# The fifth key block of the value product in high and low parts, weights widened by integer addition, and a new order of steps

## The chip, the cores and the metric

The kernel runs on one core of a Trainium2 chip, as one program. The metric is the device time of an execution in microseconds (us), the median of three runs. The engines are named as in the profile: PE (TensorE, matmul), PEld (its weight load), DVE (VectorE), ACT (ScalarE), POOL (GpSimd) and SP (SyncE, which issues most DMAs).

## The reference

Three parts stand one behind the other; the output of each is the input of the next.

```python
# q, k, v: (2, 8, 576, 64); rotary on q and k, softmax over 576 keys
scores = scale * np.matmul(q_rot, k_rot.transpose(0, 1, 3, 2))
attn = np.exp(scores - np.max(scores, axis=-1, keepdims=True))
attn = attn / (np.sum(attn, axis=-1, keepdims=True) + 1e-09)
x = np.matmul(attn, v)            # -> (1152, 512)
h = x @ w_in                      # (512, 2048), float64
x = (h * sigmoid(h)) @ w_out      # (2048, 512), float64
p = domain_probs / (domain_probs.sum(-1, keepdims=True) + 1e-09)
for e in range(4):                # w1[e]: (512, 1024), w2[e]: (1024, 512)
    out += p[:, e:e + 1] * (np.maximum(x @ w1[e], 0.0) @ w2[e])
```

## The kernel before

Every product that needs full precision is made of float32r numbers in two parts: a high part `hi` (a rounded copy) and a low part `lo` (the number less `hi`); a product is then two or three matmuls.

Attention goes over 8 pairs of heads. A pair has 9 units: four row blocks of 128 queries for each of its two heads, and one unit (h = 2) in which the last 64 queries of both heads lie together. So there are 72 iterations. In iteration `i` the kernel issues the scores of unit i + 2 (`scores`, PE, L401 to L413), their row maximum (`rowmax`, DVE, L420), the exponential of unit i + 1 (`expo`, ACT, L430), and for unit i the transposes of the probabilities (`transp`, PE, L306) with the high copy on ACT (L468) and the low subtraction on DVE (L473). Background work of neighbouring pairs is put in between: transposes of the next pair's rotated queries and keys (`qkt_*`), the product with the values (`av`), normalising (`norm`), and on POOL the rotary of the pair after next.

Three things set the order. `PLAN*` says in which of the nine iterations of a pair a background item stands. `ORDER*` is one string for each of the nine iterations: each letter issues one group of steps (S scores, M maximum, E exponential, T transposes, H high copies, L low halves, B background, v and V copies out of PSUM, X delayed steps). POOL's items are dealt out at a steady rate. Every engine runs its instructions in the order in which they were issued. `PLAN0` and `ORDER0` belong to the first pair, `PLAN2` and `ORDER2` to the last two.

The 576 keys of a head are four blocks of 128 and a fifth block of 64. For the four, `av` multiplies `P.V` (values, high in one half of the 128 columns and low in the other) with `pth` and `ptl`, the high and low parts of the transposed probabilities: eight matmuls of 256 or 320 columns (L503). The fifth block is not split: plain float32 values `V5` (64 rows for each head) and probabilities `p5`, two matmuls on 64 rows and 64 columns, each on one half of the query columns (L509). `p5` comes from one transpose into a bank of its own behind every unit with h = 1, and one copy on ACT (L470). The pool `ps1` has four PSUM banks for all of this.

The weights `w_in` and `w_out` are float64. `widen` turns the two 32-bit halves `hw` and `lw` of 512 numbers for each partition into a high and a low float32r part: 7 operations on DVE and 2 on ACT (L90 to L112). The first quarter of `w_in` is widened during attention in four slices, which start in the iterations 15, 24, 33 and 51 of `CONV` and take one stage in each iteration from there. The rest follows in the two expert stages.

Of the kernel before, what the change touches and what calls it, by code (L numbers as in the profile page):

```python
# [7 lines left out]
F32 = mybir.dt.float32  # L8
# [28 lines left out]
def fused_kernel(ctx, tc, q, k, v, w_in, w_out, dprobs, w1, w2, cst, out):  # L37
    nc = tc.nc
# [22 lines left out]
    wslot = [None] * 4  # L61

# [20 lines left out]
    def widen(cv, raw, wh, wl, slow=False):  # L83
# [33 lines left out]
        if slow:  # L117
            return [together(t0, t1), together(t2, t3, t4), t5, together(t6, t7)]
# [34 lines left out]
    pp = apool(ectx, "pp", 2)  # L153
# [10 lines left out]
    V5 = [hold5.tile([128, 64], F32, name=f"v5_{i}") for i in range(2)]  # L164
# [50 lines left out]

    def load_v5(P):
        if P.n >= 2:
            for h in range(2):
                assert (pairs[P.n - 2], "avmm", 1, h) in made
        for h in range(2):  # L220
            nc.sync.dma_start(V5[P.i][64 * h:64 * h + 64, :], v[P.b, 2 * P.hp + h, 512:576, :])
# [54 lines left out]
    def vsplit(P):  # L276
# [156 lines left out]
    def transp(P, un):  # L433
        hf, r, h = un
        if (r, h) == (P.halves[hf][0], 0):
# [4 lines left out]
                pool.tile([128, W], F32, name="p5"),  # L440
# [47 lines left out]
    def av(P, hf, h):  # L488
# [3 lines left out]
        def mm(i):  # L492
# [31 lines left out]
        return [(W / 2400, lambda i=i: mm(i)) for i in range(9)]  # L524
# [804 lines left out]
```

## Time and profile before

| | us |
|---|---|
| median of 3 runs | 766.76 (766.74 to 767.05) |
| the profiled execution | 765.77 |
| its span in the trace | 764.0 |
| PE busy | 747.0 (98%) |
| DVE busy | 508.9 (67%) |
| ACT busy | 341.7 (45%) |
| POOL busy | 286.6 (38%) |

Attention takes the first 187 us or so; the two expert stages follow. Busy shares are means over both, so they say little of either: the windows further down cut attention into pairs. Matmul records overlap (one starts before the one ahead has ended), so how long a matmul holds PE is read from the distance of two starts, not from its duration.

### The profile page before, as it was taken

The page shows a single profiled execution, that of the slowest core. Times are in us where ns is not written, and L with a number is a line of the kernel's source. Part 1 is how long each engine was busy: PE and PEld are TensorE (multiplying, and loading weights), DVE is VectorE, ACT ScalarE, POOL GpSimd, SP SyncE. Part 2 cuts the span into 40 slices and gives each one's busy share as a digit, 9 for nine tenths or more (in the row PEclk, how much of TensorE's full clock was granted, in tenths as well). Part 3 has the DMA queues.
Part 4 walks back from the last instruction along what each step waited for, and adds up shares of the span by engine and source line. Part 5 has one row for each costly group of instructions (what it writes and reads, how often), then busy time and mean ns, then how long its engine had stood idle before and what let it go on. Part 6 is the DMA issues. An engine that isn't in the chain of part 4 may idle for free.

```text
span 764.0 us, 12106 instructions
## 1 busy us (share of the span) xinstructions
PE 747.0 (98%) x4610; PEld 690.2 (90%) x4610; DVE 508.9 (67%) x936; ACT 341.7 (45%) x806; POOL 286.6 (38%) x308
## 2 busy tenths in 40 slices
PE   7998999999999999999999999999999999999998
PEld 6887878788999999999998898989989899898996
DVE  5789998987999899895565454545445454454542
ACT  4888888885533525235233242423314233141330
POOL 7997877421001303105331703426043261422600
PEclk8999999999999999999999999999999999999999
DMA  4445534230313133131110110301103030020002
GB/s 130 121 132 129 128 87 117 66 117 2 112 55 111 56 111 111 56 111 55 56 56 1 56 56 0 111 1 57 55 2 110 1 94 18 25 87 1 1 28 96
DMA packets 31129, 51.88 MB, mean 68 GB/s; under 512 B 7184, under 2 KB 14112, under 8 KB 31072
## 3 DMA queue, kind: packets, MB, share of 16 engines
q1 hardware_dynamic: 28720, 50.05, 21.6%
q10 hardware_dynamic: 2224, 0.79, 0.4%
q8 instruction: 36, 0.59, 0.3%
q0 software_dynamic: 128, 0.28, 0.1%
q14 instruction: 21, 0.17, 0.1%
HBM read 41.40 MB, written 2.36 MB: 57 GB/s over the span
## 4 chain that ended last, share of the span: by engine, by line
PE 89%; DVE 5%; POOL 2%; ACT 2%; issue 1%; DMA 1%; POOLq 0%; ACTq 0%; DVEq 0%
PE m L837 9%; PE m L838 9%; PE m L839 9%; PE m L766 7%; PE m L764 7%; PE m L765 7%; PE b L306 4%; PE m L648 4%; PE m L673 4%; PE m L649 4%; PE m L672 4%; PE m L650 4%; PE m L671 4%; PE b L503 3%; PE s L401 3%; ACT p L430 1%
## 5 line engine op out<-in xcount | busy, mean ns | idle before, releaser
L843 DVE SCALAR_TENSOR_TENSOR acc<-m,dp,acc 128x512 f32<-128x512 f32 (+1 forms) x64 | 47.5, 742 | 108.3 <-PE m L839 108.3
L838 PE MATMUL m<-wl,gh 128*128 128x512 f32 (+1 forms) x292 | 113.2, 388 | 0.0
L837 PE MATMUL m<-wh,gh 128*128 128x512 f32 (+1 forms) x292 | 113.1, 387 | 0.0
L839 PE MATMUL m<-wh,gl 128*128 128x512 f32 (+1 forms) x292 | 112.7, 386 | 0.0
L785 DVE SCALAR_TENSOR_TENSOR gl<-g,gh 128x288 fp32r<-128x288 f32 x84 | 51.2, 609 | 44.5 <-ACT gh L784 43.4
L747 POOL TENSOR_TENSOR wl<-raw,wh 128x512 fp32r<-128x512 f32 x21 | 27.2, 1295 | 141.5 <-ACT wh L744 141.5
L660 POOL TENSOR_TENSOR gl<-g,gh 128x384 fp32r<-128x384 f32 x24 | 26.9, 1121 | 141.3 <-ACT gh L659 112.7
L764 PE MATMUL m<-xh,wh 128*128 128x288 f32 x224 | 66.1, 295 | 0.0
L766 PE MATMUL m<-xh,wl 128*128 128x288 f32 x224 | 66.0, 295 | 0.0
L765 PE MATMUL m<-xl,wh 128*128 128x288 f32 x224 | 65.9, 294 | 0.0
L839 PEld LDWEIGHTS m<-wh,gl 128*128 128x128 f32 x292 | 54.9, 188 | 11.4
L837 PEld LDWEIGHTS m<-wh,gh 128*128 128x128 f32 x292 | 54.8, 188 | 10.7
L673 PE MATMUL m<-gl,wh 128*128 128x384 f32 x192 | 64.2, 334 | 0.0
L672 PE MATMUL m<-gh,wl 128*128 128x384 f32 x192 | 64.1, 334 | 0.0
L671 PE MATMUL m<-gh,wh 128*128 128x384 f32 x192 | 64.1, 334 | 0.0
L838 PEld LDWEIGHTS m<-wl,gh 128*128 128x128 f32 x292 | 54.8, 188 | 10.3
L747 POOL TENSOR_TENSOR wl<-cvt,wh 128x512 fp32r<-128x512 f32 x28 | 36.2, 1294 | 69.7 <-ACT wh L744 69.7
L420 DVE TENSOR_REDUCE nm<-s 128x1 f32<-128x576 f32 x72 | 53.9, 748 | 9.6 <-PE s L401 6.4
L744 ACT CAST wh<-cvt 128x512 fp32r<-128x512 f32 x28 | 17.4, 621 | 89.4 <-DVE cvt L743 89.4
L430 ACT ACTIVATE p<-s,nm 128x576 f32<-128x576 f32 x72 | 54.1, 751 | 5.6 <-DVE nm L420 5.0
L306 PE MATMUL b<-cs,p 128*128 128x128 f32 x329 | 50.5, 282 | 5.0 <-DVE xn L563 1.9
L473 DVE TENSOR_TENSOR ptl<-b,pth 128x512 fp32r<-128x512 f32 x72 | 48.8, 685 | 5.3 <-ACT pth L468 4.2
(179 smaller groups left out, 2094.6 us busy)
## 6 DMA issues: line engine op xcount, KB each, us to landing
raw<-in_moe_w_dram SPq DMA_DIRECT2D x16, 1024.0 KB, 5.1
raw<-in_moe_w_out_dram SPq DMA_DIRECT2D x8, 1024.0 KB, 5.0
raw<-in_moe_w_in_dram SPq DMA_DIRECT2D x6, 1024.0 KB, 5.0
kh<-kkh SPq DMA_DIRECT2D x28, 128.0 KB, 2.3
kl<-kkl SPq DMA_DIRECT2D x28, 128.0 KB, 2.3
xv<-in_v_dram SPq DMA_DIRECT2D x8, 256.0 KB, 2.7
raw<-in_moe_w_in_dram SPq DMA_DIRECT2D x4, 512.0 KB, 4.0
xk<-in_k_dram SPq DMA_DIRECT2D x7, 256.0 KB, 2.9
```

The lines of the kernel that those rows point to most:

```text
L306: nc.tensor.matmul(o, lhsT, idn[:, 0:n], is_transpose=True, start=True, stop=True)
L430: nc.scalar.activation(o.rearrange("p (a b) -> p a b", a=2), s[:, :, 0:288], AF.Exp, bias=P.nm[:, c:c + 1], scale=1.0, accum_out=P.sm[:, c ...
L671: nc.tensor.matmul(o, wh[:, f, ds], gh[:, cols], start=(f == 0), stop=False)
L672: nc.tensor.matmul(o, wl[:, f, ds], gh[:, cols], start=False, stop=False)
L673: nc.tensor.matmul(o, wh[:, f, ds], gl[:, cols], start=False, stop=(f == FT - 1))
L747: nc.gpsimd.tensor_tensor(lo, src(name), f32(hi), ALU.subtract)
L764: nc.tensor.matmul(ps, wh[:, k, ms], hh[:, k, cols], start=(first and k == 0), stop=False, skip_group_check=not first)
L765: nc.tensor.matmul(ps, wh[:, k, ms], hl[:, k, cols], start=False, stop=False, skip_group_check=not first)
L766: nc.tensor.matmul(ps, wl[:, k, ms], hh[:, k, cols], start=False, stop=(k == 1), skip_group_check=not first)
L837: nc.tensor.matmul(ps, gh[:, ts], wh[:, f, ds], start=(f == 0), stop=False)
L838: nc.tensor.matmul(ps, gh[:, ts], wl[:, f, ds], start=False, stop=False)
L839: nc.tensor.matmul(ps, gl[:, ts], wh[:, f, ds], start=False, stop=(f == FT - 1))
```

## The change

The fifth block of the product with the values is made like the other four: `P.V` gets a fifth block, into which `vsplit` puts high and low parts of `V5`, where each head has its own 64 rows and the other 64 rows are zero; `p5` gets a high and a low part for both heads' rows together, so that two matmuls of the full shape replace the two small ones. Its transposes are gathered: two row blocks at a time, into one bank, at units (1, 1) and (3, 1). The pool of probabilities `pp` has three buffers instead of two.

`widen0` is a new way to widen, for the four slices in attention alone: the low words become an integer on ACT, and one integer addition adds them to the shifted high words; 5 operations on DVE and 3 on ACT. `WIDE` says in which iteration the load and each of the six steps of a slice stand, and the new letter W issues them. The tables `PLAN*` and `ORDER*` are new; one line of each kind stands here.

```diff
-PLAN = [['Nk', 'L0'], [], ['Nq0', 'L1'], ['Ln'], ['P0'], ['Nr'], [], ['Nq1', 'P1'], ['Pn']]
+PLAN = [[], ['L0', 'Nk'], ['Nq0', 'L1'], ['Ln'], ['P0'], ['Nr', 'Nq1'], [], ['P1'], ['Pn']]
-ORDER = ['TvHSMEXVBL', 'SvTEBHVXML', 'vSTHEVMXBL', 'vSEVTBMXHL', 'THEvSVXMBL', 'vSVETHXMBL', 'vVSTEHMLXB', 'vTHSXLBEMV', 'vTSEXHVMBL']
+ORDER = ['ETvSMXHVWLB', 'BSETvVMHWXL', 'vTHEXSMLBVW', 'vESVMTHBLWX', 'vTWESHVXMBL', 'vTVSEBMHXWL', 'EvVSTHMWLXB', 'THvSXMLEWBV', 'vSVXTBMEHLW']
-CONV = [15, 24, 33, 51, 58, 61, 69]
+WIDE = [[24, 27, 27, 28, 28, 29, 32], [32, 34, 34, 36, 37, 40, 41], [41, 44, 44, 45, 46, 47, 50], [50, 52, 52, 53, 54, 55, 60]]
+CONV = [69]
-RB0 = 4
-VS = 6
-GEXTRA = 0.0
+RB0 = 5
+VS = 8
+GEXTRA = 0.5
...
+        def t0():
+            T["t"] = cv.tile([128, 512], U32, name="cvt", tag="cv")
+            T["y"] = cv.tile([128, 512], U32, name="cvy", tag="cv")
+            nc.scalar.activation(f32(T["t"]), f32(hw), AF.Abs)
+            nc.scalar.activation(T["y"][:], lw, AF.Identity, scale=2.0 ** -29, bias=big[:, 0:1])
+
+        def t1():
+            t = T["t"]
+            V.tensor_scalar(f32(t), f32(t), 2.0 ** -15, None, ALU.max)
+            V.tensor_scalar(t[:], t[:], 3, 0x3FFFFFF8, ALU.logical_shift_left, ALU.bitwise_and)
+
+        def t2():
+            V.scalar_tensor_tensor(T["t"][:], hw, 0xC0000000, T["t"][:], ALU.bitwise_and, ALU.bitwise_or)
+
+        def t3():
+            V.tensor_tensor(T["t"][:], T["t"][:], T["y"][:], ALU.add)
+
+        def t4():
+            nc.scalar.activation(wh, f32(T["t"]), AF.Copy, scale=0.5)
+
+        def t5():
+            V.scalar_tensor_tensor(wl, f32(T["t"]), 0.5, f32(wh), ALU.mult, ALU.subtract)
...
-    pp = apool(ectx, "pp", 2)
+    pp = apool(ectx, "pp", 3)
...
+        part(V5[P.i][:], lambda: P.V[:, :, 4, 0:64], lambda: P.V[:, :, 4, 64:128])
...
-        five = h > 0
-        W5 = 64 if h == 2 else 128
+        five = {(1, 1): (0, 1), (3, 1): (2, 3), (4, 2): (4,)}.get((r, h))
...
-                p5 = bank(128)
-                tr(p5, pr[:, 512:640])
+                p5 = bank(256)
+                for i, r5 in enumerate(five):
+                    tr(p5[:, 128 * i:128 * i + 128], P.plist[r5][:, 512:640])
...
             nc.vector.tensor_tensor(lo, src, f32(hi), ALU.subtract)
+            if five:
+                nc.vector.tensor_tensor(lo5, p5, f32(hi5), ALU.subtract)
...
-            if i < 8:
-                nc.tensor.matmul(T["ps"], P.V[:, h, i // 2, :], (pth, ptl)[i % 2][:, h, i // 2, 0:W],
-                                 start=(i == 0), stop=False)
-            else:
-                rows = slice(64 * h, 64 * h + 64)
-                for a in range(2):
-                    part = slice(a * W // 2, (a + 1) * W // 2)
-                    nc.tensor.matmul(T["ps"][64 * a:64 * a + 64, part], V5[P.i][rows, :], pt5[rows, part],
-                                     start=False, stop=True)
...
+            j, z = divmod(i, 2)
+            rhs = (pth, ptl)[z][:, h, j, 0:W] if j < 4 else pt5[:, z, :]
+            nc.tensor.matmul(T["ps"], P.V[:, h, j, :], rhs, start=(i == 0), stop=(i == 9))
```

What the change does to two of the engines, shown at two places. First PE, the product with the values for the second half of pair 2's queries, first head, as it is issued early in pair 3 (L503 and L509 become L535; `p_1026` and `p_1024` are the fifth block of the probabilities, `yk` the next pair's keys, `s` the scores). Before:

```order
L306 MATMUL b<-cs,yk 128x128 x4
L503 MATMUL b<-pth,V 128x320
L503 MATMUL b<-ptl,V 128x320
...
L503 MATMUL b<-ptl,V 128x320
L509 MATMUL b<-p_1026,v_0_114 64x160 x2
L401 MATMUL s<-kh_119,Q 128x288 x2
```

After:

```order
L535 MATMUL b<-pth,V 128x320
L535 MATMUL b<-ptl,V 128x320
...
L535 MATMUL b<-ptl,V 128x320
L535 MATMUL b<-p_1024,V 128x320 x2
L332 MATMUL b<-cs,yk 128x128 x4
L427 MATMUL s<-kh_120,Q 128x288 x2
```

The two matmuls with `V5` (here `v_0_114`) are gone, two of the full shape stand in their place, and the transposes of the keys moved from ahead of the product to behind it.

Second DVE at the same place of the program, from the end of pair 2 into pair 3, where both kernels widen a slice (before: L97, L100, L103, L109 and L112, behind L91 and L94 a few rows earlier; after: L98, L99, L102, L105; the lower half L111 follows further on). `nm` is the row maximum, `ptl` a lower half of the probabilities, `xu` the product with the values out of PSUM. Before:

```order
L484 RECIPROCAL rs<-rs 128x5
L97 TENSOR_SCALAR cvt<-cvt 128x512
L100 TENSOR_SCALAR cvt<-cvt 128x512
L103 SCALAR_TENSOR_TENSOR cvt<-raw_1109,cvt 128x512
L420 TENSOR_REDUCE nm<-s 128x1
L563 TENSOR_TENSOR xn<-xu,b 128x256
L473 TENSOR_TENSOR ptl<-b,pth 128x4x128
L333 TENSOR_TENSOR kkl<-b,kkh 128x512
L522 TENSOR_TENSOR xu<-b,tmp 64x320
L420 TENSOR_REDUCE nm<-s 128x1
L473 TENSOR_TENSOR ptl<-b,pth 128x4x128
L109 TENSOR_SCALAR raw_1109<-cvt 128x512
```

After:

```order
L504 TENSOR_TENSOR p_1024<-b,p_1024 128x64
L513 TENSOR_REDUCE rs<-sm_113 128x5
L515 RECIPROCAL rs<-rs 128x5
L446 TENSOR_REDUCE nm<-s 128x1
L587 TENSOR_TENSOR xn<-xu,b 128x256
L98 TENSOR_SCALAR cvt<-cvt 128x512
L99 TENSOR_SCALAR cvt<-cvt 128x512
L502 TENSOR_TENSOR ptl<-b,pth 128x4x128
L546 TENSOR_TENSOR xu<-b,tmp 64x320
L359 TENSOR_TENSOR kkl<-b,kkh 128x512
L446 TENSOR_REDUCE nm<-s 128x1
L102 SCALAR_TENSOR_TENSOR cvt<-raw_1107,cvt 128x512
```

The widening moved behind a row maximum and is cut into pieces, and the lower half of the fifth block (L504) is a new operation; the integer addition (L105, one custom operation on 1024 two-byte elements) comes right behind the last row shown.

## Rows read from the trace of the kernel before

**Rows 1.** Page, slices: PE's busy tenths in 40 equal slices.

```profile
PE   7998999999999999999999999999999999999998
```

**Rows 2.** Windows, pairs 1 to 7: PE, PEld, DVE, ACT, POOL busy (instructions); clock, DMA.

```profile
32.29:52.70 20.41, 20.14 (x162) 17.62 (x161) 17.25 (x32) 17.92 (x47) 19.75 (x23) 1.00 0.54 149
52.70:74.57 21.87, 19.98 (x152) 17.17 (x152) 21.01 (x37) 18.39 (x48) 18.11 (x19) 1.00 0.46 116
74.57:96.74 22.17, 20.40 (x157) 17.46 (x157) 21.30 (x38) 18.47 (x47) 16.53 (x18) 1.00 0.44 112
96.74:118.79 22.05, 20.25 (x155) 17.36 (x154) 20.44 (x37) 17.89 (x46) 16.59 (x18) 1.00 0.37 89
118.79:138.68 19.89, 19.78 (x158) 17.46 (x156) 16.76 (x31) 17.74 (x47) 15.34 (x19) 1.00 0.35 95
138.68:160.03 21.35, 19.98 (x155) 17.34 (x155) 19.62 (x36) 17.75 (x48) 4.61 (x8) 1.00 0.28 65
160.03:187.00 26.97, 26.71 (x199) 23.31 (x198) 19.95 (x41) 18.83 (x50) 5.74 (x11) 1.00 0.21 79
```

**Rows 3.** Waits, pairs 2 to 4: total us, times, longest us.

```profile
PE b L306 <- DVE ptl L473: 1.8, 3, 0.6
```

**Rows 4.** Timeline of PE, a product of 256 columns: start us, duration us.

```profile
88.52 0.28 PE L503 MATMUL b<-pth,V 128*128 128x256 f32 x1
...
89.35 0.28 PE L503 MATMUL b<-ptl,V 128*128 128x256 f32 x1
89.56 0.43 PE L509 MATMUL b<-p,v 64*64 64x128 f32 x4
89.92 0.40 PE L401 MATMUL s<-kh,Q 128*128 128x288 f32 x1
```

**Rows 5.** Timeline of PE, end of a product of 320 columns.

```profile
100.70 0.31 PE L503 MATMUL b<-ptl,V 128*128 128x320 f32 x1
100.94 0.49 PE L509 MATMUL b<-p,v 64*64 64x160 f32 x4
101.36 0.53 PE L401 MATMUL s<-kh,Q 128*128 128x288 f32 x2
```

**Rows 6.** Lines of the widening, 40 to 190 us: minimum, median, maximum ns.

```profile
L91 DVE TENSOR_SCALAR raw<-raw x6: 420/674/1055, 51.4 to 189.4; 128x512 uint32<-128x512 uint32 x6
L94 DVE SCALAR_TENSOR_TENSOR raw<-raw x6: 692/694/1031, 51.9 to 189.8; 128x512 uint32<-128x512 uint32 x6
L97 DVE TENSOR_SCALAR cvt<-cvt x5: 385/508/619, 55.1 to 179.8; 128x512 f32<-128x512 f32 x5
L100 DVE TENSOR_SCALAR cvt<-cvt x5: 427/510/848, 55.6 to 180.3; 128x512 uint32<-128x512 uint32 x5
L103 DVE SCALAR_TENSOR_TENSOR cvt<-raw,cvt x5: 693/733/767, 56.4 to 180.7; 128x512 uint32<-128x512 uint32 x5
L109 DVE TENSOR_SCALAR raw<-cvt x5: 423/715/828, 61.0 to 187.9; 128x512 uint32<-128x512 uint32 x5
L112 DVE SCALAR_TENSOR_TENSOR wl<-raw x5: 693/1665/1673, 61.7 to 188.4; 128x512 fp32r<-128x512 uint32 x5
```

**Rows 7.** Timeline of DVE and of POOL at the end of a slice.

```profile
106.10 1.67 DVE L112 SCALAR_TENSOR_TENSOR wl<-raw 128x512 fp32r<-128x512 uint32 x1
...
105.75 1.47 POOL L235 TENSOR_TENSOR t<-xk,cs 128x512 f32<-128x512 f32 x1
```

**Rows 8.** Groups of instructions: count, busy us, mean ns, idle before.

```profile
L90 ACT ACTIVATE cvt<-raw 128x512 f32<-128x512 f32 x32 | 21.7, 678 | 0.2 <-DMA raw<-in_moe_w_in_dram 0.2
...
L470 ACT COPY p<-b 128x128 f32<-128x128 f32 (+1 forms) x40 | 10.7, 266 | 0.0
...
L563 DVE TENSOR_TENSOR xn<-xu,b 128x256 f32<-128x256 f32 (+1 forms) x16 | 7.0, 436 | 0.0
...
L376 DVE TENSOR_TENSOR kl<-b,kh 128x128 fp32r<-128x128 f32 x7 | 2.0, 280 | 0.0
```

**Rows 9.** Timeline of POOL at the start; in brackets the idle time before.

```profile
6.51 0.72 POOL L1046 TENSOR_TENSOR t<-xk,cs 128x256 f32<-128x256 f32 x1 [2.25 <-DMA xk<-in_k_dram]
```

More of the change, by code (lines that the diff above doesn't have):

```diff
@@ L61, in fused_kernel @@
     wslot = [None] * 4
+    big = pers.tile([128, 32], F32, name="big")
     def new_slot(pool, i):
@@ L81, in fused_kernel, with widen0, widen @@
             units.append(w2[e, hf * 512:(hf + 1) * 512, :].rearrange("(t p) d -> p t d", p=128))
-    def widen(cv, raw, wh, wl, slow=False):
+    def widen0(cv, raw, wh, wl):
+        lw, hw = (raw.rearrange("p (n a) -> p n a", a=2)[:, :, a] for a in range(2))
+        T = {}
+        V = nc.vector
+        def t0():
[15 more added lines that the diff above has]
+            V.scalar_tensor_tensor(wl, f32(T["t"]), 0.5, f32(wh), ALU.mult, ALU.subtract)
+        return [t0, t1, t2, t3, t4, t5]
+    def widen(cv, raw, wh, wl):
         lw, hw = (raw.rearrange("p (n a) -> p n a", a=2)[:, :, a] for a in range(2))
@@ L163, in fused_kernel @@
     SM = [hold5.tile([128, 16, 2], F32, name=f"sm_{i}") for i in range(2)]
-    V5 = [hold5.tile([128, 64], F32, name=f"v5_{i}") for i in range(2)]
+    V5 = [hold5.tile([128, 2, 64], F32, name=f"v5_{i}") for i in range(2)]
     QR = [hold.tile([128, 384], F32R, name=f"qr_{i}") for i in range(2)]
@@ L214, in load_v @@
         )
[L216 to L219, printed above, removed]
         for h in range(2):
-            nc.sync.dma_start(V5[P.i][64 * h:64 * h + 64, :], v[P.b, 2 * P.hp + h, 512:576, :])
+            nc.sync.dma_start(V5[P.i][64 * h:64 * h + 64, h, :], v[P.b, h0 + h, 512:576, :])
     def swapped(ap):
@@ L465, in transp @@
         last = un == [u for u in P.units if u[0] == hf][-1]
+        if five:
+            n5 = 64 if h == 2 else 256
+            hi5, lo5 = (pt5[:, z, P.off[five[0]]:P.off[five[0]] + n5] for z in range(2))
         def high():
@@ L522, in evac @@
                          lambda: nc.vector.tensor_tensor(xu[own, 0:W], T["ps"][own, :], tmp[own, 0:W], ALU.add)))
-        return [(W / 2400, lambda i=i: mm(i)) for i in range(9)]
+        return [(W / 2400, lambda i=i: mm(i)) for i in range(10)]
     def rbc(P, hf):
@@ L1032, in slice0 @@
             nc.sync.dma_start(raw[:], units[0][:, t, :])
-            return widen(cv0, raw, wslot[0][0][:, t, :], wslot[0][1][:, t, :], True)
-        for t in range(FT):
-            feed.add(0, lambda t=t: slice0(t))
+            return widen0(cv0, raw, wslot[0][0][:, t, :], wslot[0][1][:, t, :])
+        steps0 = {}
         yk = pp.tile([128, 1152], F32, name="p", tag="p").rearrange("p (a e d) -> p a e d", e=2, d=64)
@@ L1099, in attention @@
         load1(pairs[1], "q", q)
+        for i in range(2):
+            g.memset(V5[i][:], 0.0)
         load_v(P0)
@@ L1169, in background, with widening @@
                 run(items)
+            def widening():
+                for t, at in enumerate(WIDE):
+                    for j, u in enumerate(at):
+                        if u == i:
+                            if j == 0:
+                                steps0[t] = slice0(t)
+                            else:
+                                steps0[t].pop(0)()
             for atom in (ORDER0 if p == 0 else ORDER if NN else ORDER2)[s]:
@@ L1199, in attention @@
                     background()
+                elif atom == "W":
+                    widening()
             if i == 0:
@@ L1224, in attention @@
             if i == 9 * (NPAIR - 1) - 1:
-                feed.need(0)
+                assert len(steps0) == FT and not any(steps0.values())
                 lctx.close()
```

28 lines of the change are left out of this document (13 added, 15 removed).

## The prediction

> **What bounds the kernel now.** I read the page's slices first: PE is busy in nine tenths or more of nearly every slice [rows 1], and from about 187 us to the end, where the two expert stages run, nothing of the change is executed. So the question is only attention, the first 187 us. There I cut the trace at every ninth exponential, which gives one window for each pair of heads [rows 2]. The reader is to see two kinds of window. In pairs 1, 5 and 7, which hold no slice of early widening, PE is busy 20.14 of 20.41, 19.78 of 19.89 and 26.71 of 26.97 us: PE sets the pace. In pairs 2, 3, 4 and 6, each of which holds one slice of weights to widen, the same PE work takes 21.87, 22.17, 22.05 and 21.35 us, PE is idle for 1.4 to 1.9 us, and DVE is busy 21.01, 21.30, 20.44 and 19.62 us: DVE sets the pace, and a widened slice costs the pair about 1.7 us against the mean of pairs 1 and 5 (20.15). Third, the waits of pairs 2 to 4 show how DVE's lateness reaches PE: a transpose has to wait for a bank of PSUM until a lower half has been subtracted [rows 3].
>
> **The fifth block on PE.** Now it is two matmuls for each product, which stand in the trace as four records on 64 rows and 64 columns. With 256 columns the first of the eight matmuls starts at 88.52 and the eighth at 89.35, 0.119 us apart; the fifth block starts 0.21 us behind the eighth, and the next other matmul 0.57 us behind it [rows 4]. In the new form the fifth block is two more matmuls of the same shape as the eight, so the next one starts three spacings behind the eighth: 0.36 us. That saves 0.21 us. With 320 columns the eighth starts at 100.70 and the next other matmul at 101.36 [rows 5]; at 0.148 us (0.119 times 320/256) three spacings are 0.44 us: 0.22 us saved. There are four such products in a pair: 0.86 us in each pair, 6.9 us in eight pairs, all of it where PE sets the pace. The number of transposes stays the same.
>
> [...]
>
> **The fifth block on the other engines.** DVE gets new work: two lower halves of 256 columns and one of 64 in each pair. The nearest rows are a subtraction out of PSUM with 256 columns, 0.436 us, and one with 128, 0.280 us [rows 8]; for 64 columns I take 0.2 us as an estimate. That is 1.07 us a pair, 8.6 us in all, and it could be 0.9 where DVE has no gaps. ACT copies two pieces of 256 in place of four of 128 (0.266 us each [rows 8]) and casts 128 columns of values: about even. POOL gets one subtraction a pair; it has 4 to 6 us free in pairs 2 to 5 [rows 2], so even one as long as the 1.47 us of [rows 7] is hidden; in pair 1, where 0.66 us is free, it would push the rotary of a later pair, for which there is a pair of slack. The two clearings at the start go into POOL's 2.25 us of waiting for the first keys [rows 9].
>
> **The widening.** A slice is seven DVE operations now. Their medians are 0.67, 0.69, 0.51, 0.51, 0.73, 0.72 and 1.67 us, together 5.5 us; their minima add up to 3.73, their maxima to 6.82 [rows 6]. The spread is POOL's doing: the 1.67 us one starts at 106.10, 0.35 us behind a POOL operation of 1.47 us, and ends some 0.5 us behind that one's end [rows 7]. In the new form there are five: maximum, mask, combination, addition, lower half. For the first three I take the medians of the same operations, 0.51, 0.51, 0.73. The lower half reads two plain inputs; between 0.69 and 1.67 us I take 0.9, nearer to the combination, which also has two inputs and keeps to 0.77 at most. The addition has no row: it is a custom operation on 1024 two-byte elements. If it goes two at a time it costs 0.69 like any two-input operation of 512 columns; if one at a time twice the 0.73, that is 1.47. I take 1.1, the middle, as no row is nearer to either. Sum 3.75, so 1.75 us less for a slice and 7.0 us less in all. The ends are 2.89 us (all at the minimum) and 5.38 us (all at the maximum). ACT gets one more pass of a slice, 0.68 us [rows 8], and has 3.5 to 4.2 us free in these pairs.
>
> So DVE as a whole gains 7.0 and pays 8.6 us; what changes is where it lies. The new table starts the four slices in iterations 24, 32, 41 and 50. Work of an iteration shows up about two exponentials later, so pair 2 loses its slice, pairs 3, 4 and 6 keep one each, and pair 5 gets one. It also hands the steps out one or two at a time instead of in three lumps of up to 2.4 us.
>
> **The sum, by pairs.** Pair 0: two products, 0.43 us, of which I count 0.3, because it starts up on POOL's rotary. Pair 1: PE sets the pace, 0.86 less. Pair 2 turns into a pair without a slice: 20.15 less 0.86 is 19.3, and with 1.07 us more on DVE I take 19.5, so 2.4 less. Pair 3: DVE 21.30 - 5.5 + 1.07 + 3.75 = 20.6; at its share of 0.96 as now, 21.5, 0.7 less. Pair 4: 20.44 - 0.68 = 19.8, at 0.94 21.0, 1.1 less. Pair 5: the DVE work of pairs 3 and 4, 20.2 at 0.96, 21.1, so 1.2 more than its 19.89. Pair 6, where POOL is nearly idle: 19.62 - 0.68 = 18.9 at 0.93, 20.35, 1.0 less. Pair 7: 0.86 less. Together 0.3 + 0.86 + 2.4 + 0.7 + 1.1 - 1.2 + 1.0 + 0.86 = 6.0 us. The rest of the kernel follows 6.0 us earlier with nothing changed: PE is full there, and its own weights are widened relative to the end of attention. The profiled execution took 765.77 us, 1.0 below the median of the three runs (766.76), so it becomes 759.8 and the median 760.8 us. Another order of steps is not in this sum; it can help or hurt.
>
> **The rivals.**
> 1. DVE stays the bound in four pairs: every new operation meets POOL and the addition costs 1.47. A slice is then 5.38 us, 1.63 more than I took, 1.7 us at a share of 0.96; in pairs 3 to 5, where POOL works, that is 5.1 us: 765.9 us, from 764 to 767. For it: the 1.67 us [rows 7]. Against it: the steps are spread out, and pair 6 has no POOL work. [...]
> 2. The new order packs the steps so well that PE sets the pace everywhere. Pairs 3 to 6 then take their PE time less 0.86 at a share of 0.985: 19.8, 19.7, 19.2 and 19.4 in place of 21.5, 21.0, 21.1 and 20.35, 5.9 us less: 754.9 us. For it: the DVE sums of pairs 4 to 6, 19 to 20 us, lie less than 1.5 us above PE's 19. Against it: two engines that are both near full leave no room for waits in a fixed order.
> 3. Small tiles were free: the PE term is zero. Pairs 0, 1 and 7 lose 2.0 us of the gain and pair 2 0.86: 763.7 us. Against it stands the gap of [rows 4].
> 4. Slower: the bank with the fifth block's transposes was free once ACT had copied it; now DVE must also read it, at the end of its iteration, and PE has four such banks. Three times a pair, 24 times in all, PE could stand at the next transpose. Today's longest wait of that kind is 0.6 us [rows 3]; at 0.6 each the cost is 14.4 us and the time 775 us, at half of it 768. It decides from 0.25 us each. Against it: two of 256 columns take the place of four banks, so fewer are in use.
>
> **How the numbers follow.** My forecast, 760.8 us (its own range 757.5 to 764), gets 0.50; rival 2 0.17, rival 1 0.17, rival 3 0.05, rival 4 0.11. Rival 1 straddles the line of 0.2% (1.5 us, about what a measurement of this kernel can tell from no change): 0.08 of it is faster, 0.09 the same. Faster: 0.50 + 0.17 + 0.05 + 0.08 = 0.80; same 0.09; slower 0.11. The range 754.5 to 766.5 leaves out rival 4 and the lower part of rival 2.
>
> **What would show it.** Right: the next matmul behind a product starts three spacings behind the eighth; pairs 1 and 7 shorter by 0.8 to 0.9 us and pair 2 below 20; five DVE operations of 3.5 to 4 us a slice; pair 5 longer than now; the expert stages as long as before. Wrong: an addition well over 1.1 us, PE waiting on the lower halves of the fifth block for more than 0.25 us each, or DVE above 95% in pairs 3 to 5 with PE idle for 2 us or more in each.

## The result and the profile after

| | before | after |
|---|---|---|
| median, us | 766.82 (766.74 to 767.05) | 759.88 (759.50 to 760.07) |
| profiled execution | 765.77 | 760.04 |
| its span | 764.0 | 758.2 |

The ratio is 0.9908 (0.9891 to 0.9926): faster by 6.9 us. The forecast was 760.8. The total agrees, but several of its terms do not, as the rows show.

The page of the changed kernel, its span, its busy times and PE's slices, beside [rows 1]:

```profile
span 758.2 us, 12013 instructions
...
PE 740.1 (98%) x4546; PEld 693.6 (91%) x4546; DVE 508.2 (67%) x953; ACT 344.9 (45%) x802; POOL 289.8 (38%) x318
...
PE   7999899999999999999999999999999999999998
```

PE's busy time fell by 6.9 us (747.0 to 740.1) and DVE's by 0.7. It would be easy to stop here and say that PE saved 6.9 us. One of the experiments has the same fall of PE's busy time and hardly any gain, so the number explains nothing by itself.

The forecast cut attention at every ninth exponential. In the new order exponentials moved against the scores, so for the comparison I cut both kernels at the first score matmul of each pair. Windows of the changed kernel, pairs 0 to 7 (columns as in [rows 2]):

```profile
11.96:28.13 16.17, 13.50 (x93) 11.57 (x92) 11.67 (x20) 13.29 (x35) 15.34 (x21) 0.95 0.36 82
28.13:48.68 20.55, 20.40 (x161) 19.42 (x162) 17.34 (x36) 18.16 (x46) 19.97 (x26) 1.00 0.54 137
48.68:66.98 18.30, 18.29 (x149) 17.60 (x148) 16.72 (x34) 17.14 (x45) 17.96 (x23) 1.00 0.52 129
66.98:89.62 22.64, 19.30 (x149) 17.57 (x148) 21.77 (x39) 19.42 (x48) 17.82 (x20) 1.00 0.47 126
89.62:110.13 20.51, 18.95 (x148) 17.54 (x147) 20.00 (x39) 19.07 (x47) 16.81 (x20) 1.00 0.47 120
110.13:131.17 21.04, 19.54 (x148) 17.60 (x147) 20.38 (x39) 19.24 (x48) 17.08 (x21) 1.00 0.38 98
131.17:150.79 19.62, 18.88 (x149) 17.55 (x148) 18.52 (x38) 18.76 (x48) 7.62 (x12) 1.00 0.31 69
150.79:171.58 20.79, 19.94 (x155) 18.17 (x154) 19.01 (x38) 18.30 (x47) 4.72 (x9) 1.00 0.27 102
```

And of the kernel before with the same cut, pair 2 (a slice) and pair 5 (none):

```profile
49.22:71.41 22.19, 20.30 (x157) 17.43 (x156) 21.30 (x37) 18.50 (x48) 18.54 (x20) 1.00 0.48 129
...
115.73:135.54 19.81, 19.70 (x157) 17.44 (x156) 15.94 (x31) 17.22 (x47) 15.50 (x20) 1.00 0.41 112
```

| pair | before | after | change | forecast |
|---|---|---|---|---|
| 0 | 17.16 | 16.17 | -1.0 | -0.3 |
| 1 | 20.03 | 20.55 | +0.5 | -0.86 |
| 2 | 22.19 | 18.30 | -3.9 | -2.4 |
| 3 | 22.15 | 22.64 | +0.5 | -0.7 |
| 4 | 22.17 | 20.51 | -1.7 | -1.1 |
| 5 | 19.81 | 21.04 | +1.2 | +1.2 |
| 6 | 21.94 | 19.62 | -2.3 | -1.0 |
| 7 | 20.90 | 20.79 | -0.1 | -0.86 |
| sum | 166.35 | 159.62 | -6.7 | -6.0 |

The first matmul of the experts is 6.8 us earlier (its weights load at 171.58 instead of 178.38), yet the span is only 5.8 us shorter. The reader should see two questions: why pair 2 runs at 18.30 us, well below every pair from 1 to 7 before (the shortest takes 19.81), and where a microsecond went behind attention.

The fifth block itself looks as forecast. PE's timeline in pair 3, end of a product of 320 columns:

```profile
72.70 0.31 PE L535 MATMUL b<-ptl,V 128*128 128x320 f32 x1
72.85 0.46 PE L535 MATMUL b<-p,V 128*128 128x320 f32 x2
73.15 0.60 PE L332 MATMUL b<-cs,yk 128*128 128x128 f32 x4
```

From the eighth matmul to the next other one 0.45 us pass, forecast 0.44, and 0.66 in [rows 5]. There was a little more to gain than the distance in [rows 5] says. At the end of attention two products stand alone between matmuls of the experts. Before, the first of these and what stands at its end:

```profile
180.58 0.30 PE L503 MATMUL b<-pth,V 128*128 128x320 f32 x1
...
181.60 0.31 PE L503 MATMUL b<-ptl,V 128*128 128x320 f32 x1
181.84 0.49 PE L509 MATMUL b<-p,v 64*64 64x160 f32 x4
182.26 0.41 PE L503 MATMUL b<-pth,V 128*128 128x320 f32 x1
182.51 0.31 PE L503 MATMUL b<-ptl,V 128*128 128x320 f32 x1
...
184.05 0.44 PE L648 MATMUL m<-xh,wh 128*128 128x384 f32 x1
```

After, the first matmul of the two products and the next one of the experts:

```profile
173.80 0.30 PE L535 MATMUL b<-pth,V 128*128 128x320 f32 x1
...
176.72 0.34 PE L672 MATMUL m<-xh,wh 128*128 128x384 f32 x1
```

The two products take 3.47 us before (180.58 to 184.05) and 2.92 after, so each saves 0.27. The first full matmul behind the small block is slow here too: its successor starts 0.25 us behind it, not 0.15 (182.26 to 182.51). So where PE sets the pace, a product saves 0.22 us and, if another product stands right behind it, 0.10 more.

The widening, DVE lines from 40 to 165 us (minimum, median and maximum ns, beside [rows 6]); each row is one source line:

```profile
L98 DVE TENSOR_SCALAR cvt<-cvt x4: 388/456/617, 73.5 to 133.6; 128x512 f32<-128x512 f32 x4
...
L99 DVE TENSOR_SCALAR cvt<-cvt x4: 426/426/1372, 74.1 to 134.1; 128x512 uint32<-128x512 uint32 x4
...
L102 DVE SCALAR_TENSOR_TENSOR cvt<-raw,cvt x4: 672/794/935, 77.7 to 136.9; 128x512 uint32<-128x512 uint32 x4
...
L105 DVE CUSTOM_DVE_ANT_0 cvt<-cvt,cvy x4: 764/1134/1670, 78.4 to 139.1; 128x1024 uint16<-128x1024 uint16 x4
...
L111 DVE SCALAR_TENSOR_TENSOR wl<-cvt,wh x4: 675/1166/1260, 87.1 to 150.4; 128x512 fp32r<-128x512 f32 x4
```

The medians add up to 3.98 us for a slice, 5.5 before, 3.75 forecast; slice by slice it is 5.50 in pair 3, then 3.96, 4.22 and 3.05. The addition, guessed at 1.1 us between 0.69 and 1.47, has a median of 1.13, but it is not one price. Two of the four, on DVE and POOL:

```profile
77.44 2.05 POOL L260 TENSOR_TENSOR t<-xk,cs 128x512 f32<-128x512 f32 x1
...
78.36 1.67 DVE L105 CUSTOM_DVE_ANT_0 cvt<-cvt,cvy 128x1024 uint16<-128x1024 uint16 x1
...
138.98 0.37 POOL L559 TENSOR_SCALAR rb<-cs,rs 128x128 f32<-128x128 f32 x1
139.13 0.76 DVE L105 CUSTOM_DVE_ANT_0 cvt<-cvt,cvy 128x1024 uint16<-128x1024 uint16 x1
```

The first starts while a POOL operation runs that ends at 79.49, and ends 0.54 us behind that; the second starts while a shorter one runs that ends at 139.35, and again ends 0.54 us behind it. The other two end 0.55 us behind the end of the POOL operation that runs when they start, and so do all additions of the experiments that start like this (29 in eight traces with these four, 0.54 to 0.55). Three additions, in e8_wo and e9_w_spread, start while POOL does nothing, and take 0.67 to 0.68; the shortest of e9_w_spread is one of them:

```profile
L105 DVE CUSTOM_DVE_ANT_0 cvt<-cvt,cvy x4: 681/1154/1652, 80.7 to 141.9; 128x1024 uint16<-128x1024 uint16 x4
```

So the forecast's first case (0.69) is the price, and what comes on top lasts until 0.54 to 0.55 us behind POOL's end: that its middle of 1.1 met the median was luck. In [rows 7], too, the operation ends 0.55 us behind POOL's. Why it does, no run shows.

### The profile page after: what moved, and what is told of

The parts are those of the page before. It is cut to its first block, busy times and chain, and to the rows that moved or that the text cites. A ratio compares the mean times of both kernels' runs of the same rounds, so it can differ in the third digit from the quotient of the medians.

```text
span 758.2 us, 12013 instructions
## 1 busy us (share of the span) xinstructions
PE 740.1 (98%) x4546; PEld 693.6 (91%) x4546; DVE 508.2 (67%) x953; ACT 344.9 (45%) x802; POOL 289.8 (38%) x318
## 4 chain that ended last, share of the span: by engine, by line
PE 86%; ACT 7%; DVE 6%; issue 1%; DMA 1%; ACTq 0%; DVEq 0%; POOLq 0%
PE m L862 9%; PE m L861 9%; PE m L863 9%; PE m L790 7%; PE m L789 7%; PE m L788 7%; PE m L672 4%; PE m L674 4%; PE m L673 4%; PE m L696 4%; PE m L695 4%; PE m L697 4%; PE b L332 3%; PE b L535 3%; ACT p L456 3%; PE s L427 2%
```

## The experiments

The change has four parts, counting one that its words do not name. F is the fifth block, with the third buffer of `pp`, earlier loads of `V5` and a keyword at the building of the program that the words do not name either (`dynamic_dma_scratch_size=8192`), none of which ran by itself; W the integer addition (not the letter W of the tables); O the order (the tables, the times of the slices and the handing out of POOL's items); and P a shift of the weights in SBUF, which comes with the new tile `big`. Eleven kernels ran, in three groups (e1 to e4, e5 to e8, e9 to e11), each beside the kernel before, whose medians were 766.53, 766.59 and 766.44 us. The intervals of the ratios are about 0.1 to 0.2% to each side, so steps of less than 1 us between two kernels rest on runs that do not overlap, where I name them.

### e1_align: the new tile 256 bytes long instead of 128

```diff
-    big = pers.tile([128, 32], F32, name="big")
+    big = pers.tile([128, 64], F32, name="big")
```

> The changed kernel with one edit: the constant tile that stands ahead of the weight buffers takes 256 bytes of a row instead of 128, so the weights and the hidden values of the expert stages lie 128 bytes further on. In the trace of the changed kernel three matmuls of the first product of the expert stages (hidden from x and weights) take 0.53 us, before 0.52 us; 240 such triples are 1.9 us. Theory, the place in memory: the triple goes back to 0.52 us, attention ends at the same time, total 758.0 us (757.5 to 758.6). Rival, the rate differs from execution to execution or from chip to chip: total as the changed kernel's, 759.9 us, with a triple of 0.53 us here too.

758.45 us (757.95 to 758.75), ratio 0.9895 (0.9881 to 0.9910). All runs are below all runs of the changed kernel: 1.4 us gained by 128 bytes that nothing reads.

### e2_shift: the kernel before with 128 unused bytes ahead of the weights

```diff
     wslot = [None] * 4
+    pers.tile([128, 32], F32, name="big")
```

> The kernel before with 128 unused bytes put ahead of the weight buffers, nothing else. Theory, the place in memory: the triple of the first product goes from 0.52 to 0.53 us, attention ends at 178.4 us as before, total 1.9 us more than before (768.7 us). Rival, rate of the execution or of the chip: total as before, 766.8 us.

768.15 us (767.80 to 768.75), ratio 1.0021 (1.0012 to 1.0030): 1.6 us lost. It names the part P by itself.

### e10_x_too: x moved by 128 bytes as well

```diff
+    pers.tile([128, 32], F32, name="pad")
     xh2 = pers.tile([128, 4, NT], F32R, name="xh")
...
-    big = pers.tile([128, 32], F32, name="big")
+    big = pers.tile([128, 64], F32, name="big")
```

> The changed kernel with x (both parts) 128 bytes further on and the weights 256 bytes further, so that both start at even multiples of 128 bytes; before, and in the kernel with 256 bytes ahead of the weights, both were odd, in the changed kernel x is odd and the weights are even. Theory, the two must agree: a triple of the first product takes 0.52 us, expert stages 1.3 us shorter, total 758.5 us. Rival, the weights' own place counts: triple 0.53 us as in the changed kernel, total 759.9 us.

758.08 us (757.93 to 758.77), ratio 0.9891 (0.9875 to 0.9908). Here, in e1_align and in the kernel before, x and the weights lie an even number of 128-byte steps apart, counting only what the new tiles add; in the changed kernel and in e2_shift an odd number. x itself moved by one step here and the time stayed at e1_align's. So in these five kernels the time goes with how the two lie to one another, not with where each lies.

The groups of one of the three matmuls of the first expert product, with 384 columns. In the changed kernel:

```profile
L673 PE MATMUL m<-xl,wh 128*128 128x384 f32 x96 | 32.4, 338 | 0.0
```

In e1_align:

```profile
L673 PE MATMUL m<-xl,wh 128*128 128x384 f32 x96 | 32.1, 334 | 0.0
```

In e2_shift:

```profile
L650 PE MATMUL m<-xl,wh 128*128 128x384 f32 x96 | 32.4, 338 | 0.0
```

In e10_x_too:

```profile
L674 PE MATMUL m<-xl,wh 128*128 128x384 f32 x96 | 32.1, 334 | 0.0
```

A record of 0.34 us reaches past the next start, which comes 0.18 us behind its own, so the distance of starts must bear the difference out. Twenty triples without a pause, the first and the last start in the changed kernel's timeline:

```profile
179.82 0.34 PE L672 MATMUL m<-xh,wh 128*128 128x384 f32 x1
...
190.38 0.34 PE L672 MATMUL m<-xh,wh 128*128 128x384 f32 x1
```

And in e1_align:

```profile
179.27 0.34 PE L672 MATMUL m<-xh,wh 128*128 128x384 f32 x1
...
189.67 0.33 PE L672 MATMUL m<-xh,wh 128*128 128x384 f32 x1
```

10.56 against 10.40 us: 0.528 and 0.520 a triple. There are 240 such triples, which makes 1.9 us; the three comparisons of medians give 1.4 to 1.8. That is the microsecond lost behind attention.

### e3_fw_old: F and W, with the old order

```diff
-WIDE = [[24, 27, 27, 28, 28, 29, 32], [32, 34, 34, 36, 37, 40, 41], [41, 44, 44, 45, 46, 47, 50], [50, 52, 52, 53, 54, 55, 60]]
-CONV = [69]
+CONV = [15, 24, 33, 51, 58, 61, 69]
...
+            z = widen0(cv0, raw, wslot[0][0][:, t, :], wslot[0][1][:, t, :])
+            both = lambda a, b: lambda: [a(), b()]
+            return [both(z[0], z[1]), both(z[2], z[3]), z[4], z[5]]
```

> The changed kernel with the tables of before: the fifth block in two parts and the integer addition stay, the four slices start in iterations 15, 24, 33 and 51 as before, with the steps of a slice in four consecutive iterations. Theory, as in the prediction's sum, that the order itself is worth little: pairs 1, 5 and 7 shorter by 0.86 us, pairs 2, 3, 4 and 6 by 0.7 us, pair 0 by 0.3: 5.7 us less of attention, which ends near 172.7 us; total 761 us. Rival, the order carries the gain: attention ends behind 175 us, total 763.5 us or more.

765.58 us (765.16 to 766.26), ratio 0.9988 (0.9980 to 0.9997). The page's busy times:

```profile
PE 740.7 (97%) x4546; PEld 693.9 (91%) x4546; DVE 507.8 (66%) x953; ACT 345.3 (45%) x802; POOL 289.8 (38%) x318
```

PE's busy time is within 0.6 us of the changed kernel's, and nearly all of the gain is missing. Three short windows of pair 2 say what became of part of it:

```profile
52.00:54.00 2.00, 0.00 (x0) 0.00 (x0) 0.90 (x1) 1.61 (x3) 1.83 (x3) 1.00 0.49 145
54.00:56.00 2.00, 1.20 (x7) 0.99 (x8) 1.90 (x4) 1.95 (x7) 0.46 (x1) 0.93 0.00 0
56.00:58.00 2.00, 2.00 (x10) 1.98 (x10) 1.94 (x6) 1.91 (x6) 1.59 (x3) 0.50 0.00 0
```

PE does nothing from 52 to 54 us, little until 56, and then, from 56 to 58 us, the granted clock stands at 0.50. What PE waits for stands in ACT's timeline of the same kernel:

```profile
52.39 0.68 ACT L92 ACTIVATE cvt<-raw 128x512 f32<-128x512 f32 x1 [1.86 <-DMA raw<-in_moe_w_in_dram]
...
53.62 0.57 ACT L378 ACTIVATE Q<-b 128x512 fp32r<-128x512 f32 x1
```

The first step of a slice waits 1.86 us for its weights, and the copy of the queries that the scores need is queued behind it. SP issues this load at 48.56 us, 1.4 us later than in the kernel before (47.18, where the step waits 0.21 us), because the new form of the fifth block puts its two loads of values (1.12 us of SP's time) ahead of it instead of behind. Pair 2 takes 23.79 us; the next pairs, with the same work, 21.41 and 21.37. The new table starts each slice's load two or three iterations ahead of its first step, and in the changed kernel's waits of attention this load does not appear.

### e4_f_new: F and O, with the old widening in six steps

```diff
+        if slow:
+            return [t0, together(t1, t2), together(t3, t4), t5, t6, t7]
...
-            return widen0(cv0, raw, wslot[0][0][:, t, :], wslot[0][1][:, t, :])
+            return widen(cv0, raw, wslot[0][0][:, t, :], wslot[0][1][:, t, :], True)
```

> The changed kernel with the widening of before (7 operations on DVE, 2 on ACT) put into the same six steps and iterations; fifth block and new order stay. Theory, DVE sets the pace of the pairs that hold a slice: a slice took 5.65 us on DVE before and 4.18 us in the changed kernel, so four of them cost 1.5 us each: attention ends near 177.5 us, total 765.8 us. Rival, with the steps spread out PE sets the pace and DVE has room: attention ends before 173 us, total 761 us or less.

765.49 us (764.20 to 767.35), ratio 0.9988 (0.9980 to 0.9997). In the new order the old widening costs 5.6 us more than the integer addition. The profiled execution was the longest, 767.35; six us of its pair 5:

```profile
122.00:125.00 3.00, 1.36 (x7) 1.40 (x7) 2.96 (x6) 2.21 (x6) 1.27 (x3) 0.52 0.37 80
125.00:128.00 3.00, 3.00 (x14) 2.98 (x14) 3.00 (x5) 1.67 (x4) 2.83 (x4) 0.50 0.65 145
```

Again PE stood (1.36 of 3 us busy, as in the 3 us ahead of these), DVE was full (2.96 and 3.00 of 3 us), and the granted clock was 0.52 and then 0.50. The pair took 24.96 us, 21.04 in the changed kernel. So the 5.6 us hold more than DVE's additional work.

### e5_f_old: F alone, with the old widening and order

```diff
+            return [together(t0, t1), together(t2, t3, t4), t5, together(t6, t7)]
...
+            return widen(cv0, raw, wslot[0][0][:, t, :], wslot[0][1][:, t, :], True)
```

> The fifth block in two parts alone: widening and tables of before (the weight buffers keep the changed kernel's places, so the expert stages take 1.3 us more than before). Theory, DVE pays for it where it sets the pace: 1.07 us more in pairs 2, 3, 4 and 6, 0.86 us less in pairs 1, 5 and 7 and 0.3 in pair 0; attention ends 1 to 2 us later than before (178.4), total 768 to 770 us. Rival, PE's saving passes everywhere: attention ends at 172 to 174 us, total 762 to 764 us.

769.68 us (769.50 to 769.95), ratio 1.0040 (1.0025 to 1.0055). The fifth block alone makes the kernel slower: by 1.5 us against e2_shift, which has the weights at the same place. But one stall makes it so: pair 2 has that of e3_fw_old again.

```profile
52.71 0.69 ACT L121 ACTIVATE cvt<-raw 128x512 f32<-128x512 f32 x1 [2.09 <-DMA raw<-in_moe_w_in_dram]
```

The pair's window:

```profile
48.91:73.71 24.80, 20.57 (x150) 19.05 (x148) 22.61 (x40) 18.63 (x47) 19.73 (x23) 0.93 0.50 130
```

Pairs 3 and 4, with the same work, take 22.57 and 22.56 us, so some 2.2 us of pair 2 are the stall and the lower clock behind it (0.56 from 56 to 59 us, 0.93 in the pair's mean). Without them, as an estimate from these pairs, the fifth block would have gained 0.7 us here. The theory's 1.07 us more in a pair with a slice is not there either: pairs 3 and 4 are 0.4 us longer than before.

### e6_w_old: W alone

```diff
+            z = widen0(cv0, raw, wslot[0][0][:, t, :], wslot[0][1][:, t, :])
+            both = lambda a, b: lambda: [a(), b()]
+            return [both(z[0], z[1]), both(z[2], z[3]), z[4], z[5]]
```

> The integer addition alone: fifth block and tables of before, five DVE operations in place of seven in the same four iterations of a slice (weights 128 bytes further, 1.3 us more in the expert stages). Theory, DVE sets the pace of the four pairs with a slice: 1.5 us less in each, attention ends at 172.5 to 173.5 us, total 762 us. Rival, a fixed order turns DVE's spare time into waits of PE, as it seems to be with both parts and the old tables (attention ended at 177.1): attention ends behind 176 us, total 765.5 us or more.

765.59 us (764.89 to 768.81), ratio 0.9990 (0.9979 to 1.0001); against e2_shift 2.6 us less.

### e7_o_only: O alone

The new tables and the letter W; widening and fifth block as before, and no `big`.

```diff
+            return [t0, together(t1, t2), together(t3, t4), t5, t6, t7]
...
+                elif atom == "W":
+                    widening()
```

> The new tables alone: fifth block as before, the seven operations of the old widening put into the new iterations (weights at their old places). Theory, the spreading of the slices is worth something by itself, since pairs 2 and 4 lose lumps of DVE work: attention ends 1 to 3 us earlier, total 764 to 765.5 us. Rival, the tables fit only the changed steps: attention ends later than 178.4 us, total 767 us or more.

767.49 us (765.39 to 768.26), ratio 1.0004 (0.9994 to 1.0013): nothing gained. In its profile, its longest execution, pair 5 takes 24.85 us at a mean granted clock of 0.86; pair 2, which has lost its slice, takes 18.81.

### e8_wo: W and O, with the old fifth block

```diff
-            j, z = divmod(i, 2)
-            rhs = (pth, ptl)[z][:, h, j, 0:W] if j < 4 else pt5[:, z, :]
...
+                for a in range(2):
+                    part = slice(a * W // 2, (a + 1) * W // 2)
+                    nc.tensor.matmul(T["ps"][64 * a:64 * a + 64, part], V5[P.i][rows, :], pt5[rows, part],
+                                     start=False, stop=True)
```

> The changed kernel with the fifth block of before: integer addition and new tables stay (weights at the changed kernel's places). What it loses against the changed kernel is what the fifth block is worth. Theory, 0.2 us for each of 32 products on PE, less where DVE sets the pace: attention ends 3 to 5 us later than the changed kernel's 171.6, total 763 to 765 us. Rival, the three lower halves on DVE eat the saving: attention ends before 173 us, total 761.5 us or less.

761.14 us (761.02 to 761.33), ratio 0.9928 (0.9914 to 0.9943). Most of the gain is here, without the fifth block; all its runs are above those of the changed kernel, by 1.3 us at the median. Its pair 2, which has no slice:

```profile
49.60:68.45 18.85, 18.85 (x157) 17.16 (x156) 15.95 (x31) 17.10 (x46) 16.53 (x20) 1.00 0.52 137
```

### e9_w_spread: W with the slices at the new times, otherwise the old order

```diff
+WIDE = [[24, 27, 27, 28, 28, 29, 32], [32, 34, 34, 36, 37, 40, 41], [41, 44, 44, 45, 46, 47, 50], [50, 52, 52, 53, 54, 55, 60]]
...
             feed.tick(i in CONV)
+            widening()
```

> The integer addition with the fifth block and the tables of before, but the six steps of a slice in the changed kernel's iterations (27 to 60, at the end of each iteration) instead of four stages in four iterations. So far: integer addition in the old places, attention ends at 175.8 us; integer addition with the new tables, 172.0 us. Theory, it is the spreading of the slices that lets PE keep its pace: attention ends at 172 to 173.5 us, total 761 to 763 us. Rival, it is the order of the other steps and of the background work: attention ends at 175 us or later, total 764.5 us or more.

763.76 us (763.59 to 764.17), ratio 0.9966 (0.9953 to 0.9979): 1.8 us less than e6_w_old, 2.6 more than e8_wo. The order's worth lies partly in when the slices run and partly in the rest of the tables, and the run settles for neither alone. Of the 2.6 us, 1.6 lie in pair 5 (21.96 us here, 20.39 in e8_wo) and 0.9 in pair 2. Its pair 2:

```profile
49.08:68.84 19.76, 19.65 (x158) 17.39 (x156) 15.92 (x30) 17.06 (x46) 16.58 (x20) 1.00 0.47 126
```

The same matmuls as in e8_wo's pair 2, no slice in either, PE busy all but 0.1 us in both, and 0.9 us between them. The share of PEld tells the two apart: 17.39 of 19.76 us is 0.88, 17.16 of 18.85 is 0.91. Some of the 0.9 us can be read from the starts. Three of the four products here stand right behind transposes, and their second matmul starts 0.23 to 0.25 us behind the first; in e8_wo one does, and in the others it starts after 0.12 to 0.15: 0.2 us in all. One set of scores starts 0.38 us behind the transpose ahead of it instead of 0.11, and only 0.11 of that is counted as idle, because the record of a transpose lasts 0.27 us.

### e11_no_lo5: the changed kernel without the lower halves of the fifth block

```diff
-            if five:
-                nc.vector.tensor_tensor(lo5, p5, f32(hi5), ALU.subtract)
...
-            rhs = (pth, ptl)[z][:, h, j, 0:W] if j < 4 else pt5[:, z, :]
+            rhs = (pth, ptl)[z][:, h, j, 0:W] if j < 4 else pt5[:, 0, :]
```

> The changed kernel without the 24 lower-half subtractions of the fifth block on DVE; the matmuls that would read the lower halves read the high halves again, so PE's work is the same and only the fifth block's lower part is wrong. Theory, DVE pays for the fifth block in the pairs that hold a slice: 1.07 us less in each of pairs 3 to 6, attention ends 3 to 5 us earlier than 171.6, total 755 to 757 us. Rival, other waits hold the pairs by now (ACT is busy 93% there): less than 1 us, total 759 us or more.

757.02 us (756.86 to 757.43), ratio 0.9879 (0.9864 to 0.9893). (The high halves are added twice here, so more than the lower part differs; the work on PE is the same.) The 24 subtractions on DVE, 1.05 us of work in a pair, cost 2.9 us: between the two expectations. The theory's place is wrong: every pair from 1 to 7 is shorter by 0.15 to 0.72 us, and most of all pairs 2 and 7, which hold no slice (0.50 and 0.72). Pairs 2 and 3:

```profile
48.57:66.37 17.80, 17.80 (x150) 17.53 (x148) 16.03 (x31) 17.11 (x45) 17.46 (x22) 1.00 0.53 127
66.37:88.68 22.31, 18.92 (x150) 17.55 (x148) 21.02 (x36) 19.39 (x48) 18.91 (x21) 1.00 0.50 138
```

Against e8_wo's 18.85 the fifth block on PE alone is worth 1.05 us in pair 2, 0.26 for each product, as the tail of attention had it. With the lower halves on DVE, 0.55 of that is left (18.30). In pairs 3 to 5 the changed kernel is 0.5, 0.45 and 0.65 us longer than e8_wo (22.13, 20.06, 20.39). Without the lower halves they are still 0.15 to 0.2 us longer (22.31, 20.20, 20.58): there PE's saving gains nothing.

Where the lower halves cost time shows in the waits. In the changed kernel the first weight load of 12 products waits for a lower half on DVE, 3.8 us in all; one of them:

```profile
83.99 0.19 PEld L535 LDWEIGHTS b<-pth,V 128*128 128x128 f32 x1 [0.49 <-DVE ptl L502]
```

In e11_no_lo5 one such wait is left:

```profile
PEld b L533 <- DVE ptl L502: 0.2, 1, 0.2
```

In pair 2 of the changed kernel there are two, of 0.21 and 0.25 us, and the pair is 0.50 us longer than in e11_no_lo5. Why already the first matmul waits, which reads only a high half, no run shows.

### The runs together

One ladder from the kernel before to the best version; steps are differences of medians.

| kernel | us | step |
|---|---|---|
| before, beside e2_shift | 766.53 | |
| + P (e2_shift) | 768.15 | +1.6 |
| + W (e6_w_old) | 765.59 | -2.6 |
| + the new times of the slices (e9_w_spread) | 763.76 | -1.8 |
| + the rest of O (e8_wo) | 761.14 | -2.6 |
| + F (after) | 759.88 | -1.3 |
| - P (e1_align) | 758.45 | -1.4 |

The parts are not worth the same on another rung. F: +1.5 us on P alone, 0.0 on P and W (e3_fw_old), both with the stall of pair 2; -1.3 on P, W and O; some -3.6 on O (e7_o_only to e4_f_new, with 1.6 taken for P, and runs of both spread over 3 us). W: -2.6 on P, -4.1 on P and F (e5_f_old to e3_fw_old), -5.6 on P, F and O (e4_f_new to after). O alone gains nothing (e7_o_only); it brings 4.4 us on P and W, 4.2 on P and F, 5.7 on P, F and W. e1_align and e10_x_too beat both kernels; between these two, 758.45 and 758.08, the runs do not decide.

## Why the prediction was right or wrong

**The total** was right by luck, by terms that made up for one another: 6.0 us forecast, 6.9 measured. Two of the forecast's own signs of being right failed (pairs 1 and 7 are not 0.8 us shorter, and the expert stages are longer), and its signs of being wrong were met in part: waits for lower halves of 0.32 us in the mean, and in pair 3 DVE at 96% with PE idle for 3.3 us.

**"PE sets the pace" in pairs 1, 5 and 7** failed. It rested on PE busy for 19.78 of 19.89 us [rows 2]. The same matmuls run in 18.85 us in e8_wo's pair 2, after another ordering alone (19.76 in e9_w_spread), and in 18.81 in e7_o_only's. So there were 0.9 us in a "full" PE, which its busy share doesn't show, because a record lasts longer than the distance to the next start (0.31 us against 0.15 in a product of 320 columns) and hides a short wait. The busy share of the weight loads tells these windows apart: 0.88 in pair 5 before, 0.91 in e8_wo's pair 2, 0.96 in the changed kernel's, 0.98 in e11_no_lo5's. How much is to be had the share does not say: between e9_w_spread and e8_wo the weight loads' time is nearly the same, and only the window is shorter.

**"Another order of steps is not in this sum"** left out the largest term: 4.4 us on the ladder, 1.8 from the times of the slices and 2.6 from the rest. On the ladder this is not the clock: from pair 1 on no pair of e6_w_old, e9_w_spread, e8_wo and the changed kernel has a granted clock below 1.00 in its profile. (e6_w_old was profiled in its shortest execution; its others show a mean clock down to 0.993, so of the 1.8 us a part may be it.) Off the ladder it counts: an idle PE and the lower clock behind it stand in pair 2 of e3_fw_old and e5_f_old (0.93 in the mean of the pair), with the old order, and in pairs 4 and 5 of e4_f_new (0.93 and 0.86) and pair 5 of e7_o_only (0.86), with the new order and the old widening. What else the order mends inside PE's pipeline is taken apart only for pair 2, and there not to the end.

**The fifth block on PE** was sized too small where PE leads, 0.22 us a product against 0.26 to 0.27 measured (tail of attention, e11_no_lo5), and too large as a gain: 6.9 us forecast, 1.3 on the ladder. The step that failed is the one that let it count in full in pairs 1 and 7, nearly so in 0 and 2, and set DVE's new work against the widening's alone, without a wait of PE. The 1.07 us a pair were right (two of 0.415 and one of 0.215), but they cost 2.9 us at the end, where the products wait for a lower half: 0.50 us in pair 2 and 0.72 in pair 7, where the forecast had put down nothing or hardly anything. And in pairs 3 to 5 PE's saving brings nothing even without them.

**The widening**: 3.98 us by the medians against 3.75, 4.18 in the mean. The addition's 1.13 against 1.1 is luck: 0.68 alone, the rest until 0.54 to 0.55 us behind POOL's end. With old tables that brings 2.6 us, not 7.0, as in the sum's own step most of it was to be spent again on DVE.

**The pairs.** Pair 2 as a pair without a slice is right in kind (18.30 us against 19.5), pair 5's extra slice in size too (+1.2). Pair 3 is wrong in sign: DVE has 21.77 us of work there, 20.6 forecast, one addition of 1.67 us and the longest mask (L99 up to 1.37 us) among it. Pair 1 is wrong in sign because work moved into it from pair 0: 161 matmul records instead of 157, though the fifth block takes 8 from a pair, and 93 in pair 0 instead of 106; the two together gained 0.5 us of the 1.16 forecast. Of pair 7's gain most stands behind its window, in the tail (0.55 us), and 0.72 us went to the lower halves. Pair 0 gained more than forecast, with a mean granted clock of 0.95 in place of 0.89.

**"The rest of the kernel follows 6.0 us earlier with nothing changed"** failed by 1.4 to 1.8 us: nothing in its instructions changed, but the place of its weights did.

**The rivals.** Rival 1 is right that every addition of the changed kernel met POOL, but its price came in pair 3 only (5.50 us for the slice, 5.38 in the rival; 3.05 to 4.22 in the others). Rival 2 has right that the order is worth something: with P taken out, the kernel stands at 758.1 to 758.5, between the forecast and its 754.9. What it rests on, PE setting the pace everywhere, did not come about in pairs 3 to 5, where PE is idle for 3.3, 1.6 and 1.5 us. Rival 3 is refuted by the tail rows and e11_no_lo5: 0.27 and 0.26 us for each product in place of its zero. Rival 4's wait is real, at another place; waits of attention in the changed kernel:

```profile
PEld b L535 <- DVE ptl L502: 3.8, 12, 0.5
PE b L332 <- DVE ptl L502: 3.8, 6, 1.5
```

Transposes waited 3.8 us in six places, up to 1.5, for a lower half (beside [rows 3]; 2.2 us in four places over the whole of attention before). But in e11_no_lo5, without the fifth block's halves, they wait 4.9 us in eight places, so the bank that the rival named isn't the cause. What the fifth block's halves add is the first row, the products' wait, 12 times 0.32 us (0.8 us in two places before). That is half of the 24 waits at which the rival decides, and without the halves the kernel is 2.9 us faster: a loss, but not the whole of the gain.

## What to carry to other kernels

Before a "full" PE is called the bound, look at the share of its weight loads and at the same matmuls in another stretch or order: here 99% busy still held 0.9 us in 20 (weight loads 0.88 of the window; 0.91 in the shorter one). Price a new engine operation on the kernel as it will be, not as it is, since the fifth block was worth +1.5, 0 or -1.3 us depending on what ran beside it; and look for what it moves: in the old order a load that came 1.4 us later in its queue cost 2.2 us. And after adding a tile, compare stages that the change doesn't touch: 128 bytes in front of the weights took back a fifth of the gain.

## What of the hardware was not expected

- **The place of two operands.** With x and the weights moved against one another by 128 bytes in each partition (the changed kernel), a triple of 384-column matmuls took 0.528 instead of 0.520 us; moved by 256 bytes (e1_align), it took 0.520 again. Products with 288 columns keep their 295 ns and the weight loads their 188 ns in both kernels. Why the place counts, no run shows.
- **A short wait cost twice.** In e3_fw_old PE stood for some 3 us of 52 to 56, and the granted clock then fell to 0.50: pair 2 took 2.4 us longer than pairs 3 and 4 with the same work, 1.3 of it idle and 1.1 in PE's longer busy time (20.4 instead of 19.3 us). This is one reason why the parts' gains don't add up.
- **One instruction, one price and a wait.** The integer addition of 1024 two-byte elements took 0.67 to 0.68 us in the three cases in which POOL did nothing. Where a POOL operation ran at its start it ended 0.54 to 0.55 us behind that operation's end, in all 29 cases, so it lasted from 0.76 to 1.67 us in the changed kernel.
